# Linear attention and two feed-forward layers on one core: the stores of y1 move from SP's queue to ScalarE's, and the stores of converted weights are written one tile later

## The chip, the cores and the metric

The kernel runs on one core of one Trainium2 chip. The metric is device time of one execution in microseconds, the median of several runs. A core has a matrix engine (TensorE, PE in the rows), a vector engine (VectorE, DVE), a scalar engine (ScalarE, ACT), GpSimd (POOL) and SyncE (SP), which here only issues DMAs. Each engine works through its own queue in order; an instruction that waits holds up all that is queued behind it on the same engine.

## What is computed

The reference, cut to its core:

```python
for t in range(S):                                   # B, H, S, D = 4, 8, 768, 64
    state = gamma[None, :, None, None] * state + np.einsum('bhd,bhe->bhde', k[:, :, t], v[:, :, t])
    y[:, :, t] = scale * np.einsum('bhd,bhde->bhe', q[:, :, t], state)
x = y.transpose(0, 2, 1, 3).reshape(B * S, H * D)    # 3072 tokens of 512
h = x @ w_in                                         # 512 -> 1024
e = np.exp(h - h.max(-1, keepdims=True))
solu = h * e / (e.sum(-1, keepdims=True) + 1e-09)
ln = (solu - mean(solu)) / sqrt(var(solu) + 1e-06) * g_ln
x = ln @ w_out                                       # 1024 -> 512, this is y1
h = x @ w2_in                                        # 512 -> 2048
out = (h * np.cos(h)) @ w2_out                       # 2048 -> 512
```

The weights of the four matrices arrive as 64-bit floats, as pairs of 32-bit words, and are turned into 32-bit floats on the chip.

## The kernel before

Attention is done in 24 steps (two pairs of batches, 12 chunks of 64 positions each). `load_step` issues six loads a step on SP (`kt`, two of `X`, two of `W`, `kn`); `att_prep` scales `kn` on ScalarE in four operations (L223); the rest of a step is short matmuls on TensorE.

The first layer works on tiles of 128 tokens. `mm1` makes `h` in PSUM in two halves of 12 matmuls (L315); there is one buffer for `h`, so the next tile's matmuls wait until the norm has read it. `norm` is a chain over three engines: row maximum on VectorE (L323), exp on ScalarE (L324, tile `u`), `u*h` on VectorE (L325), sum of squares on ScalarE (L328, tile `junk`), small arithmetic on VectorE and GpSimd (L327 to L335, tiles `sm`), and a scaling on ScalarE (L336, tile `u` again). `transp` turns the normed tile by eight transposes on TensorE (L351, tile `tr`, two buffers), and each `tr` is split on ScalarE (`lth`, L354) and VectorE (`ltl`, L355). `mm2` multiplies with the second matrix (48 matmuls, L368) for 256 tokens and half of the 512 outputs; behind every second call a copy on ScalarE (`ys`, L372, one buffer) empties PSUM and a DMA on SP (L373) stores it to `y1d` in DRAM. There are 24 such stores. The second layer reads `y1d` back with `load_y`.

While the first layer runs, the weights of both layers are converted: `load_w` loads a tile of word pairs on SP (`raw`, L155), takes an absolute value on ScalarE (`wt`, L158) and does four operations on VectorE (L161, L162, L164, L167). Tiles of the second layer have no room yet, so `keep` stores them to DRAM on SP (L191, 28 stores, tensors `kept_in` and `kept_out`), and `load_kept` reads them back later. There are two `wt` buffers.

One round of the main loop (`for s in range(EARLY, NG)`) does two tiles of `mm1`, one group of `transp` and `mm2`, one or two attention steps and four calls of `weights`. TensorE's order is the order of the program text. The order on the other engines is set by a scheduler when the program is built, from modelled times; the text gives it only what depends on what.

Of the kernel before, what the change touches and what calls it, by code (L numbers as in the profile page):

```python
# [50 lines left out]
def body(ctx: ExitStack, tc: tile.TileContext, qx, kt, kn, vn, c_sc, c_mg,  # L51
         w_in1, w_out1, gln, w_in2, w_out2, out):
    nc = tc.nc
# [10 lines left out]
    y1d = [dram.tile([128, KD, 512], F32, name=f"y1d{n}") for n in range(NBLK)]  # L64
# [59 lines left out]
    def split(hi, lo, src, pin=False, head=None):  # L124
        op = nc.scalar.activation(out=hi, in_=src if head is None else head, func=AF.Copy)  # L125
        if pin:
            tc.keep_in_program_order(op)
        nc.vector.tensor_tensor(out=lo, in0=src, in1=hi.bitcast(F32), op=ALU.subtract)  # L128
# [13 lines left out]
    def load_w(src, apart=False):  # L142
        seq[0] += 1
        if early:
            raw = early.pop(0)
            src = None
            t = p_boot.tile([128, 512], I32, tag="wt", name="wt", bufs=4)
        elif "lt" not in p2 and seq[0] % 2:
            raw = p2["boot"].tile([128, 512, 2], I32, tag="raw", name="raw", bufs=3)
            t = p2["boot"].tile([128, 512], I32, tag="wt", name="wt", bufs=2)  # L150
        else:
            raw = stg.tile([128, 512, 2], I32, tag="raw", name="raw", bufs=3)
            t = stg.tile([128, 512], I32, tag="wt", name="wt")
        if src is not None:
            nc.sync.dma_start(out=raw, in_=src.rearrange("p (f two) -> p f two", two=2))  # L155
        f = t.bitcast(F32)
        top, low = raw[:, :, 1], raw[:, :, 0]
        first_op = nc.scalar.activation(out=f, in_=top.bitcast(F32), func=AF.Abs)  # L158
        if seq[0] > 2 * KD:
            tc.keep_in_program_order(first_op)  # L160
        nc.vector.tensor_scalar(out=f, in0=f, scalar1=TINY, scalar2=HUGE, op0=ALU.max, op1=ALU.min)  # L161
        nc.vector.tensor_scalar(out=t, in0=t, scalar1=3, scalar2=0x3FFFFFFF,  # L162
                                op0=ALU.logical_shift_left, op1=ALU.bitwise_and)
        nc.vector.scalar_tensor_tensor(out=t, in0=top, scalar=-0x40000000, in1=t,  # L164
                                       op0=ALU.bitwise_and, op1=ALU.bitwise_or)
        full = low if apart else t
        nc.vector.scalar_tensor_tensor(out=full, in0=low, scalar=29, in1=t,  # L167
                                       op0=ALU.logical_shift_right, op1=ALU.bitwise_or)
        return (f, full.bitcast(F32)) if apart else f
# [15 lines left out]
    w2h, w2l = {}, {}  # L185
    kept = {}

    def keep(kind, c, e, k, src):
        if k == 0:
            kept[kind, c, e] = dram.tile([128, 2, 512], F32, name=f"kept_{kind}_{c}_{e}")  # L190
        nc.sync.dma_start(out=kept[kind, c, e][:, k], in_=load_w(src))  # L191

    def load_kept(what, hi, lo):
        t = stg.tile([128, 2, 512], F32, tag="raw", name="raw", bufs=3)
# [164 lines left out]
    def mm2(g, p, e):  # L359
        if e == 0:  # L360
            y1s[g] = p2["pst"].tile([128, 2, 256], F32, tag="y1", name="y1")
        y1 = y1s[g]
        ds = slice((2 * p + e) * 128, (2 * p + e + 1) * 128)
        m = 0
        for j in range(K1):
            lh, ll = lt[g][j // 2]
            for w, a in ((o1[0], lh), (o1[1], lh), (o1[0], ll)):
                nc.tensor.matmul(out=y1[:, e], lhsT=w[:, j, ds], rhs=a[:, j % 2], start=(m == 0), stop=(m == 3 * K1 - 1))  # L368
                m += 1
        if e == 1:  # L370
            ys = moe.tile([128, 2, 256], F32, tag="ys", name="ys", bufs=1)
            nc.scalar.activation(out=ys, in_=y1, func=AF.Copy)  # L372
            nc.sync.dma_start(out=y1d[g // 2][:, 2 * p:2 * p + 2, (g % 2) * 256:(g % 2) * 256 + 256], in_=ys)  # L373


    def load_y(n):
        yh = p2["sb"].tile([128, KD, 512], F32R, tag="yh", name="yh")
        yl = p2["sb"].tile([128, KD, 512], F32R, tag="yl", name="yl")
        for k in range(KD):
            t = p2["sb"].tile([128, 512], F32, tag="yt", name="yt", bufs=2)  # L380
            nc.sync.dma_start(out=t, in_=y1d[n][:, k])
            split(yh[:, k], yl[:, k], t)
        p2["y", n] = (yh, yl)
# [45 lines left out]
    def load_o2(g):  # L429
# [7 lines left out]
        for e in range(2):  # L437
# [4 lines left out]
    wq = [(load_w1, (k, c)) for c in range(2) for k in range(KD)] + [(load_o1, (j,)) for j in range(K1)]  # L442
    wq += [(load_w2, (p_w2a, 0, k)) for k in range(KD)]
    wq += [(keep, ("in", 1, k // 2, k % 2, w_in2[k * 128:(k + 1) * 128, 1024:2048])) for k in range(KD)]
    wq += [(keep, ("out", 0, j // 2, j % 2, w_out2[j * 128:(j + 1) * 128, :])) for j in range(K2)]
    wq += [(keep, ("in", c, k // 2, k % 2, w_in2[k * 128:(k + 1) * 128, c * 1024:(c + 1) * 1024]))
           for c in (2, 3) for k in range(KD)]

    def weights(n):
        for _ in range(n):  # L450
            if wq:
                f, args = wq.pop(0)
                f(*args)
# [83 lines left out]
    for s in range(EARLY, NG):  # L537
        g = s - EARLY
        first(2 * s, 0)
        transp(g, 0)  # L540
        transp(g, 1)
        first(2 * s, 1)
        transp(g, 2)
        transp(g, 3)
        if s < NG - 1:
            attend()
        weights(1)
        for e in range(2):
            mm2(g, 0, e)
        weights(1)  # L550
        first(2 * s + 1, 0)
        first(2 * s + 1, 1)
        weights(1)
        if s % 2 == 0:
            attend()
        for e in range(2):
            mm2(g, 1, e)
        weights(1)
    weights(len(wq))
    load_y(0)  # L560
    nup = 0
    for g in range(NG - EARLY, NG):
        transp(g, 0)
        transp(g, 1)
        up(0, nup)
        transp(g, 2)
        transp(g, 3)
        for e in range(2):
            mm2(g, 0, e)
        load_w2(None, 1 + g - (NG - EARLY), 0)  # L570
        load_o2(g - (NG - EARLY))
        up(0, nup + 1)
        nup += 2
        load_w2(None, 1 + g - (NG - EARLY), 1)
        for e in range(2):
            mm2(g, 1, e)
# [90 lines left out]
```

## Time and profile before

| | us |
|---|---|
| median of 3 runs | 931.36 |
| the runs | 929.67 to 933.35 |
| span of the profiled execution (no other time of it is given) | 932.8 |
| TensorE busy (matmuls) | 893.4 |
| VectorE busy | 622.7 |
| ScalarE busy | 455.5 |
| GpSimd busy | 48.0 |
| chain that ended last, share of TensorE | 84% |

Times within the profile are microseconds from the first instruction. The first layer's main loop runs from about 93 us to 378 us; the y1 stores are issued between 113.8 and 417.5 us. "Idle before" in a row is the time for which the engine had nothing to do ahead of that instruction, with what ended it. A wait is put down to what came last. The y1 stores carry 256 KB each, a weight load 512 KB, a kept store 256 KB.

### The profile page before, as it was taken

To read this page: it belongs to the slowest core of one execution; us is meant where nothing else is said; L and a number is where in the kernel's file an instruction comes from. 1 tells how busy PE (TensorE), PEld (TensorE's weight loads), DVE (VectorE), ACT (ScalarE), POOL (GpSimd) and SP (SyncE) were. 2 spreads that over 40 slices of the span, in tenths; PEclk is the share of its full clock that TensorE was granted. 3 is DMA by queue.
4 is the path that set the end of the run, shared out by engine and by line. 5 is a ranking of instruction groups with operands and counts; after the bars stand their busy time and mean duration, and the time that the engine had idled before them with its cause. 6 is when DMAs were issued, how large, how long until landed. Compare 5 with 4: busy or idle time off the path is not lost.

```text
span 932.8 us, 16044 instructions
## 1 busy us (share of the span) xinstructions
PE 893.4 (96%) x6464; PEld 765.1 (82%) x6464; DVE 622.7 (67%) x1090; ACT 455.5 (49%) x768; POOL 48.0 (5%) x60
## 2 busy tenths in 40 slices
PE   4787999989899999999999999999999999999997
PEld 4676889879799989998888888888888888888886
DVE  6899887587667754566766655756575665656654
ACT  4677666556656555554534333433443343344332
POOL 2112100101011000000000000000000000000000
PEclk7999899989999999999999999999999999999999
DMA  9986354565547422133012002000300030001001
GB/s 260 313 252 194 106 158 146 184 204 161 188 131 226 157 93 90 64 108 111 24 35 56 1 1 73 19 0 1 91 1 1 7 84 1 1 24 45 1 1 46
DMA packets 41884, 85.28 MB, mean 91 GB/s; under 512 B 5457, under 2 KB 11729, under 8 KB 41809
## 3 DMA queue, kind: packets, MB, share of 16 engines
q1 hardware_dynamic: 41376, 83.91, 30.0%
q8 instruction: 51, 0.84, 0.4%
q10 hardware_dynamic: 432, 0.34, 0.1%
q14 instruction: 25, 0.20, 0.1%
HBM read 64.30 MB, written 19.92 MB: 90 GB/s over the span
## 4 chain that ended last, share of the span: by engine, by line
PE 84%; DVE 6%; DMA 5%; ACT 2%; issue 2%; SPq 1%; POOL 0%; DVEq 0%; ACTq 0%
PE h L393 28%; PE acc L418 28%; PE y L368 13%; PE h L315 10%; DMA kn<-kn_dram 3%; PE tr L351 2%; PE y L287 2%; DMA W<-vn_dram 1%; PE sc L230 1%; DVE X L248 1%; DVE wt L164 1%; DVE wt L161 1%; ACT kn L223 1%; ACT junk L328 1%; DVE wt L162 0%
## 5 line engine op out<-in xcount | busy, mean ns | idle before, releaser
L393 PE MATMUL h<-yh,w2h 128*128 128x512 f32 x384 | 149.6, 390 | 0.0
L393 PE MATMUL h<-yl,w2h 128*128 128x512 f32 x384 | 149.4, 389 | 0.0
L393 PE MATMUL h<-yh,w2l 128*128 128x512 f32 x384 | 149.4, 389 | 0.0
L418 PE MATMUL acc<-o2h,gh 128*128 128x512 f32 x384 | 149.4, 389 | 0.0
L418 PE MATMUL acc<-o2h,gl 128*128 128x512 f32 x384 | 149.4, 389 | 0.0
L418 PE MATMUL acc<-o2l,gh 128*128 128x512 f32 x384 | 149.4, 389 | 0.0
L404 ACT ACTIVATE r<-r,hp 128x512 f32<-128x512 f32 x96 | 69.5, 724 | 144.5 <-DVE r L403 144.5
L368 PE MATMUL y<-lth,o1h 128*128 128x256 f32 x384 | 110.2, 287 | 0.0
L368 PE MATMUL y<-ltl,o1h 128*128 128x256 f32 x384 | 108.8, 283 | 0.0
L368 PE MATMUL y<-lth,o1l 128*128 128x256 f32 x384 | 108.6, 283 | 0.0
L401 DVE SCALAR_TENSOR_TENSOR r<-ki,h 128x512 f32<-128x512 int32 x96 | 66.0, 687 | 62.9 <-ACT ki L400 61.9
L405 DVE TENSOR_TENSOR r<-r,h 128x512 f32<-128x512 f32 x96 | 66.0, 687 | 61.6 <-ACT r L404 61.6
L128 DVE TENSOR_TENSOR gl<-r,gh 128x512 fp32r<-128x512 f32 x96 | 66.3, 691 | 45.9 <-ACT gh L125 45.4
L400 ACT ACTIVATE ki<-h 128x512 int32<-128x512 f32 x96 | 57.3, 597 | 74.7 <-PE h L393 74.1
L125 ACT ACTIVATE gh<-r 128x512 fp32r<-128x512 f32 x96 | 60.7, 632 | 65.4 <-DVE r L405 65.4
L393 PEld LDWEIGHTS h<-yh,w2h 128*128 128x128 f32 x384 | 72.1, 188 | 14.9
L418 PEld LDWEIGHTS acc<-o2h,gl 128*128 128x128 f32 x384 | 72.1, 188 | 15.0
L393 PEld LDWEIGHTS h<-yl,w2h 128*128 128x128 f32 x384 | 72.1, 188 | 15.0
L418 PEld LDWEIGHTS acc<-o2l,gh 128*128 128x128 f32 x384 | 72.1, 188 | 14.9
L418 PEld LDWEIGHTS acc<-o2h,gh 128*128 128x128 f32 x384 | 72.0, 188 | 14.9
L393 PEld LDWEIGHTS h<-yh,w2l 128*128 128x128 f32 x384 | 72.1, 188 | 14.8
L315 PE MATMUL h<-w1h,xh 128*128 128x512 f32 x192 | 77.9, 406 | 0.0
(77 smaller groups left out, 1554.3 us busy)
## 6 DMA issues: line engine op xcount, KB each, us to landing
raw<-w_in_dram SPq DMA_DIRECT2D x24, 512.0 KB, 4.4
raw<-w_out_dram SPq DMA_DIRECT2D x24, 512.0 KB, 4.8
kt<-kt_dram SPq DMA_DIRECT2D x24, 256.0 KB, 4.9
X<-qx_dram SPq DMA_DIRECT2D x48, 128.0 KB, 5.0
W<-vn_dram SPq DMA_DIRECT2D x48, 128.0 KB, 4.6
kn<-kn_dram SPq DMA_DIRECT2D x24, 256.0 KB, 5.1
y1d<-ys SPq DMA_DIRECT2D x24, 256.0 KB, 2.1
yt<-y1d SPq DMA_DIRECT2D x24, 256.0 KB, 2.9
```

What stands on the lines that cost most here:

```text
L125: op = nc.scalar.activation(out=hi, in_=src if head is None else head, func=AF.Copy)
L128: nc.vector.tensor_tensor(out=lo, in0=src, in1=hi.bitcast(F32), op=ALU.subtract)
L287: nc.tensor.matmul(out=y[64 * par:64 * par + 64, j], lhsT=d["W"][:, par, j], rhs=d["X"][:, par, j], start=True, stop=True)
L315: nc.tensor.matmul(out=h[:, c], lhsT=a[:, k], rhs=w[:, k, cs], start=(k + m == 0), stop=(k == KD - 1 and m == 2))
L351: nc.tensor.transpose(out=tr[:, e, t * 128:(t + 1) * 128], in_=lns[2 * g + t].rearrange("p c f -> p (c f)")[:, j * 128:(j + 1) * 128], ide ...
L368: nc.tensor.matmul(out=y1[:, e], lhsT=w[:, j, ds], rhs=a[:, j % 2], start=(m == 0), stop=(m == 3 * K1 - 1))
L393: nc.tensor.matmul(out=h, lhsT=w[:, k, cs], rhs=a[:, k], start=(m == 0), stop=(m == 3 * KD - 1))
L400: nc.scalar.activation(out=ki, in_=h, func=AF.Identity, scale=INV2PI, bias=0.25)
L401: nc.vector.scalar_tensor_tensor(out=r, in0=ki, scalar=-C1, in1=h, op0=ALU.mult, op1=ALU.add)
L404: nc.scalar.activation(out=r, in_=r, func=AF.Sin, bias=hp[:, 0:1])
L405: nc.vector.tensor_tensor(out=r, in0=r, in1=h, op=ALU.mult)
L418: nc.tensor.matmul(out=acc, lhsT=a[:, ts_], rhs=w, start=(j == 0 and m == 0), stop=(j == K2 - 1 and m == 2))
```

## The change

The store of y1 is issued by ScalarE, behind the copy `ys` that fills the tile, where SP issued it. And `keep` no longer stores a tile as soon as it is converted: it puts the store on a list, which is emptied at the start of the next call of `keep` and once at the end of the loop.

```diff
+    held = []
+
+    def flush_kept():
+        while held:
+            dst, t = held.pop(0)
+            nc.sync.dma_start(out=dst, in_=t)
+
     def keep(kind, c, e, k, src):
         if k == 0:
             kept[kind, c, e] = dram.tile([128, 2, 512], F32, name=f"kept_{kind}_{c}_{e}")
-        nc.sync.dma_start(out=kept[kind, c, e][:, k], in_=load_w(src))
+        flush_kept()
+        held.append((kept[kind, c, e][:, k], load_w(src)))
...
             nc.scalar.activation(out=ys, in_=y1, func=AF.Copy)
-            nc.sync.dma_start(out=y1d[g // 2][:, 2 * p:2 * p + 2, (g % 2) * 256:(g % 2) * 256 + 256], in_=ys)
+            nc.scalar.dma_start(out=y1d[g // 2][:, 2 * p:2 * p + 2, (g % 2) * 256:(g % 2) * 256 + 256], in_=ys)
...
     weights(len(wq))
+    flush_kept()
     load_y(0)
```

The lines behind the new function stand 8 lower in the changed kernel (L336 is L344, L372 is L380), and a kept store is L193 where it was L191. TensorE's order and GpSimd's are the same in both.

ScalarE at store 5, in the round that runs from 158 us to 192 us, before (the number behind a name tells one buffer or tile from another):

```order
L255 ACTIVATE W<-S 64x512
L256 ACTIVATE W<-S 64x512
L158 ACTIVATE wt<-raw 128x512
L223 ACTIVATE kn<-kn,cs 128x128 x4
L328 ACTIVATE junk,sm_123<-u,sm_123 128x1024
L372 ACTIVATE ys<-y_2125 128x512
L158 ACTIVATE wt<-raw 128x512
L336 ACTIVATE u<-u,sm_123 128x1024
L125 ACTIVATE xh<-x_1566 128x512
```

and now:

```order
L263 ACTIVATE W<-S 64x512
L264 ACTIVATE W<-S 64x512
L158 ACTIVATE wt<-raw 128x512
L231 ACTIVATE kn<-kn,cs 128x128 x4
L336 ACTIVATE junk,sm_123<-u,sm_123 128x1024
L380 ACTIVATE ys<-y_2124 128x512
L344 ACTIVATE u<-u,sm_123 128x1024
L381 DMA y1d_73<-ys 128x2x256
L158 ACTIVATE wt<-raw 128x512
L125 ACTIVATE xh<-x_1566 128x512
```

The second weight conversion (`wt`) stood right behind `ys` and stands now behind `u` and the store. The same move is made at stores 3, 9 and 13 (at 3 the store stands ahead of `u`). At stores 7 and 11 the first of the four `kn` scalings goes ahead of `junk`. On VectorE the split of a `w2` tile changes places with its neighbour three times, and one `ltl` near the end of the loop; all else there stays.

SP in the same round, before:

```order
L191 DMA kept_out_0_2115<-wt 128x512
L373 DMA y1d_73<-ys 128x2x256
L155 DMA raw<-w_out_dram 128x1024
L191 DMA kept_out_0_2115<-wt 128x512
L155 DMA raw<-w_out_dram 128x1024
L91 DMA kt<-kt_dram 128x512
L98 DMA kn<-kn_dram 128x512
```

and now:

```order
L193 DMA kept_out_0_2114<-wt 128x512
L155 DMA raw<-w_out_dram 128x1024
L193 DMA kept_out_0_2114<-wt 128x512
L155 DMA raw<-w_out_dram 128x1024
L91 DMA kt<-kt_dram 128x512
L98 DMA kn<-kn_dram 128x512
```

The y1 store has gone; the kept stores stand where they stood, ahead of the next weight load. With the y1 stores left out, SP's whole queue is the same in both kernels.

## Rows read from the trace of the kernel before

**Rows 1.** The page: the span.

```profile
span 932.8 us, 16044 instructions
```

**Rows 2.** TensorE's waits, 100 to 420 us: total us, times, longest us.

```profile
PE tr L351 <- DVE ltl L355: 7.6, 5, 4.1
```

**Rows 3.** Busy time by stretch: stretch, length, TensorE busy, granted clock, DMA share, GB/s.

```profile
190.00:193.00 3.00, 2.81 (x32) 0.50 0.92 281
250.00:253.00 3.00, 2.46 (x78) 1.00 0.95 287
260.00:420.00 160.00, 160.00 (x1416) 1.00 0.39 123
```

**Rows 4.** SP's waits over the span: total us, times, longest us.

```profile
SPq L373 <- ACT ys L372: 110.4, 20, 10.9
SPq L191 <- DVE wt L167: 74.9, 24, 9.0
```

**Rows 5.** Timeline of SP: start us, us, engine, line, operation, out<-in.

```profile
126.99 0.38 SPq L373 DMA_DIRECT2D y1d<-ys  x1
129.09 0.33 SPq L155 DMA_DIRECT2D raw<-w_in_dram  x1
...
171.96 0.32 SPq L191 DMA_DIRECT2D kept_out<-wt  x1
...
173.33 0.42 SPq L98 DMA_DIRECT2D kn<-kn_dram  x1
...
219.21 0.32 SPq L191 DMA_DIRECT2D kept_out<-wt  x1
...
232.64 0.32 SPq L191 DMA_DIRECT2D kept_out<-wt  x1
```

**Rows 6.** Timeline of ScalarE, its queue included; idle time before in brackets.

```profile
1.17 0.45 ACTq L109 DMA_DIRECT2D cs<-c_sc_dram  x1
...
142.21 0.65 ACT L158 ACTIVATE wt<-raw 128x512 f32<-128x512 f32 x1
143.18 1.25 ACT L336 ACTIVATE u<-u,sm 128x1024 f32<-128x1024 f32 x1 [0.32 <-DVE sm L335]
...
168.30 0.60 ACT L372 ACTIVATE ys<-y 128x512 f32<-128x512 f32 x1
168.79 0.65 ACT L158 ACTIVATE wt<-raw 128x512 f32<-128x512 f32 x1
169.76 1.25 ACT L336 ACTIVATE u<-u,sm 128x1024 f32<-128x1024 f32 x1 [0.32 <-DVE sm L335]
...
181.22 1.28 ACT L223 ACTIVATE kn<-kn,cs 128x128 f32<-128x128 f32 x4 [5.68 <-DMA kn<-kn_dram]
...
226.53 1.29 ACT L223 ACTIVATE kn<-kn,cs 128x128 f32<-128x128 f32 x4 [2.58 <-DMA kn<-kn_dram]
...
241.03 1.28 ACT L223 ACTIVATE kn<-kn,cs 128x128 f32<-128x128 f32 x4 [3.67 <-DMA kn<-kn_dram]
...
257.32 1.15 ACT L328 ACTIVATE junk<-u,sm 128x1024 bf16<-128x1024 f32 x1 [1.49 <-DVE sm L327]
...
259.62 1.29 ACT L223 ACTIVATE kn<-kn,cs 128x128 f32<-128x128 f32 x4 [1.06 <-DMA kn<-kn_dram]
```

**Rows 7.** Timeline of VectorE.

```profile
145.26 1.22 DVE L323 TENSOR_REDUCE sm<-h 128x1 f32<-128x1024 f32 x1
...
156.06 0.69 DVE L355 TENSOR_TENSOR ltl<-tr,lth 128x512 fp32r<-128x512 f32 x1
```

**Rows 8.** Timeline of TensorE: the two gaps.

```profile
190.10 1.11 PE L351 MATMUL tr<-ident,u 128*128 128x128 f32 x4 [4.15 <-DVE ltl L355]
...
249.92 0.66 PE L351 MATMUL tr<-ident,u 128*128 128x128 f32 x4 [1.82 <-DVE ltl L355]
```

**Rows 9.** Chain of waits, 153 to 158 us: start us, us, what.

```profile
153.40 0.87 PE tr L351 x8
154.28 2.74 PE h L315 x12
```

## What the change should do to the time

> **What bounds the kernel now.** The page comes first, for the span of 932.8 us [rows 1]. Then the view of TensorE's waits, which says where a gain or a loss can lie: in all of the stretch in which y1 is stored and weights are kept (113 us to 418 us) TensorE waits only for the second half of a transpose pair, `tr` for `ltl`, 7.6 us in five waits, the longest 4.1 us [rows 2]. The busy times by stretch show the rest: from 260 us on TensorE is busy without a break, so nothing the change does there can gain; it could only open new gaps [rows 3]. Behind the 4.15 us wait that ends at 190.10 TensorE ran at the lower of its two levels (granted 0.50, that is 1.2 GHz, in 190 to 193 us), behind the 1.82 us wait at 249.92 it did not (1.00 in 250 to 253 us) [rows 3, 8]. The whole stake on the gain side is thus 7.6 us of waits and some 1.5 us of slow work (3 us at half speed; an estimate from those rows).
>
> **SP, where the stores leave.** SP's own waits look like a large prize: 110.4 us in 20 waits for `ys` at the y1 store [rows 4]. The timeline of SP takes it back. The store at 126.99 had waited for `ys`, but the next in the queue, the weight load at 129.09, waits for a conversion on VectorE and would have stood there in any case [rows 5]. It is so at each of these stores: behind it stands either a load that needs a buffer or a kept store that needs the end of a conversion (74.9 us in 24 waits [rows 4]). What SP really gets back is 24 issues, 0.38 us each [rows 5]. The Trainium skill, "DMA: Bandwidth & Descriptors", section "Issuing engines are not separate DMA queues", says that starting DMAs from several engines saves only the sequencer's time to start them. By that rule SP's relief is 24 x 0.38 = 9 us of SP's own time and none on the path; by the 110.4 us row alone one would have credited the whole 7.6 us of TensorE's waits, and the queue's order here sides with the rule. I credit nothing.
>
> **The kept stores.** The order of SP shows them where they were, each right ahead of the next weight load; this half moves nothing and costs nothing. The scheduler, not the text, sets that order.
>
> **ScalarE, where the stores go.** Two things happen there. First, each y1 store is an instruction in ScalarE's queue: the issue takes 0.45 us (the three DMAs that ScalarE issues at the start [rows 6]), and it must wait until `ys` is finished, which costs another 0.1 us, since ScalarE otherwise starts the next operation 0.49 us into the 0.60 us copy (168.30 and 168.79). So some 0.6 us for what follows, if it was back to back. Second, the order around it changes, as the two fences on the change show: at four places (stores 3, 5, 9 and 13 of 24) the weight conversion `wt`, which stood right behind `ys`, now stands behind `u` (L336 before), and `u` must wait for a small chain on VectorE and GpSimd. At 142.21 the conversion ran while `u` waited until 143.18; now it starts at 143.18 + 1.15 = 144.33, 2.1 us later. At 168.79 and 169.76 the store is behind `u` as well: 169.76 + 1.25 + 0.45 = 171.45, 2.65 us later [rows 6]. At two more places (stores 7 and 11) one of four `kn` scalings goes ahead of `junk`.
>
> **Who waits for it.** On VectorE the four conversion operations keep their place ahead of the row maximum (L323), which opens the norm chain. At 145.26 L323 began straight behind them, so it begins at 147.3 [rows 7]. The whole chain behind it (exp, `u`, `junk`, then on ScalarE `ys`, `u`, two `wt`, two `lth`) is back to back and shifts by 2.0 us, and with it the two `ltl`, the second of which began at 156.06. TensorE wants the first at 157.02, where its 12 matmuls end, and the second 0.43 us later (half of eight transposes) [rows 7, 9]. The second now ends at 156.06 + 0.69 + 2.0 = 158.75, against 157.45: a new wait of **1.3 us**.
>
> At store 5 there is a second victim. SP's kept store at 171.96 waits for the end of the late conversion, and behind it stand a load, `kt` and `kn`, issued at 173.33; the conversion ends 2.5 us later, so the kept store goes to 174.46 [rows 5]. `kn` is what ScalarE stands for until 181.22 with 5.68 us of idle time [rows 6], and that is the wait behind the 4.15 us gap of TensorE. In other rounds `kn` was used 7.3 us (219.21 to 226.53) to 8.4 us (232.64 to 241.03) after the kept store ahead of it [rows 5, 6]; so here at 181.8 to 182.9, later by 0.6 to 1.7 us. I take 1.1, and 0.2 for the store that stands between `ys` and the second `wt` in the chain behind: **1.3 us**. At store 9 the same: kept store 232.64 to 235.1, `kn` at 242.4 to 243.5 instead of 241.03, middle 1.9, with 0.2: **2.1 us**. That makes a wait of 1.8 into one of 3.9, close to the one after which the clock fell; I count the fall, **1.5 us** as above.
>
> Store 13 repeats store 3 without `kn` (**1.3 us**). Store 11 gets there another way: `junk`, which ran at 257.32, stands behind a `kn` that lands at 259.62 [rows 6]; less what `u` used to wait anyhow and plus the issue, the conversion is 1.8 us late, and the result is that of store 3 (**1.2 us**). At store 7 it is 0.6 us, which the slack there covers. Where only the store comes in between, ScalarE's idle time hides it, save at the first two stores, whose 0.6 us goes straight into the wait that TensorE already has before 130 us (**0.7 us**), and at stores 15 and 16, which leave **0.5 us**. The last eight stores fall where TensorE waits for nothing and ScalarE waits for TensorE; nothing.
>
> **Sum.** 0.7 + 1.3 + 1.3 + 2.1 + 1.5 + 1.2 + 1.3 + 0.5 = 9.9 us, or 8.4 without the clock. The profiled span, 932.8 us, is 1.4 us above the median of the runs, 931.36, and inside their spread of 929.67 to 933.35; the page gives no time of that execution beside its span. I add the difference to the median: **941.3 us**.
>
> **Bounds.** Of the eight terms four are differences of a shift and a slack; with a microsecond more slack in each and no fall of the clock some 4.5 us are left (936). With `kn` at its late ends (1.2 us more), a slow stretch twice as long and a second one, 14.1 us are reached (945.5). The price of an issue on ScalarE in mid-program isn't in the trace; between nothing and twice 0.45 us it moves the sum by about 2 us either way, since the order is what costs.
>
> **Rivals.**
> (a) Hidden: the late conversions are made up before TensorE asks. For it: TensorE waits for nothing after 260 us today [rows 3], so there is slack in many rounds. Against: the `ltl` slack at 157.45 is 0.7 us, less than the 2.0 us that come. Price 0 to 4 us: 931 to 935.5.
> (b) Faster: with the outputs on ScalarE's queue SP runs ahead, `kn` lands before ScalarE wants it, and the waits and the slow clock go: 931.36 - 7.6 - 1.5 = 922. The point that decides is whether `kn` is issued earlier in its round than at 173.33 [rows 5]; against it, the kept store ahead of it in SP's order waits for a conversion that is now later. The Trainium skill, "Perfetto Trace Analysis", section "DMA Optimizations", suggests one DMA-capable engine for inputs and another for outputs, which would be this gain. No row here shows it: after each y1 store the queue waits for VectorE.
> (c) Worse: more of the gaps grow past the length at which the clock falls, each 1.5 us and up, over 946.
> (d) The change does nothing to the order of loads and stores of kept weights. That is half of my reading already and is priced at nothing.
>
> **Chances.** Forecast 0.62, (a) 0.20, (b) 0.08, (c) 0.10. The range 931 to 946 holds the forecast and nearly all of (a), and leaves out (b) and (c). A measurement of this kernel can tell about 0.5% from no change, 4.7 us here: slower by more than that (over 936) 0.70, within it 0.23, faster 0.07.
>
> **What would show it.** Right: in the profile of the changed kernel `tr` waits for `ltl` in eight or more places, some 15 us in all instead of 7.6; ScalarE's conversion at store 5 begins behind `u` and the store; `kn` in that round is issued 2 us or more later after the attention block than before; a stretch at 1.2 GHz near 250 us. The y1 stores show as issues on ScalarE of 0.4 us. Wrong: SP's waits for `ys` gone and `kn` issued earlier, or L323 beginning no later behind the block of matmuls it reads; or the new waits there, but each eaten by a shorter one behind it.

## The result and the profile after

The changed kernel takes 941.84 us (median of 4 runs, 940.99 to 946.14), the kernel before 931.48 us beside it (4 runs, 929.67 to 933.35): a ratio of 1.0125, 95% interval 1.0096 to 1.0154, or 10.4 us more. The forecast was 941.3. One of the ten runs of `e1_hold_only` further down took 2271.66 us and is no part of that kernel's ratio.

The page of the changed kernel, its span and the engines' busy times:

```profile
span 939.6 us, 16035 instructions
...
PE 898.0 (96%) x6464; PEld 767.4 (82%) x6464; DVE 622.7 (66%) x1090; ACT 455.9 (49%) x768; POOL 48.3 (5%) x60
```

No engine got more work; TensorE's 4.6 us more of busy time are the same matmuls at a lower clock (below). TensorE's waits, 100 to 420 us (total us, times, longest us), against 7.6 us in five waits in [rows 2]:

```profile
PE tr L359 <- DVE ltl L363: 11.1, 9, 4.4
PE h L323 <- DVE sm L337: 0.3, 1, 0.3
```

The gaps on TensorE's timeline (start us, us, ..., idle before in brackets), as in [rows 8], and the busy times by stretch (stretch, length, busy, granted clock, DMA share, GB/s), as in [rows 3]:

```profile
130.01 0.66 PE L359 MATMUL tr<-ident,u 128*128 128x128 f32 x4 [1.49 <-DVE ltl L363]
...
192.40 0.91 PE L359 MATMUL tr<-ident,u 128*128 128x128 f32 x4 [4.42 <-DVE ltl L363]
...
253.29 0.66 PE L359 MATMUL tr<-ident,u 128*128 128x128 f32 x4 [2.42 <-DVE ltl L363]
...
312.14 1.25 PE L359 MATMUL tr<-ident,u 128*128 128x128 f32 x8 [0.99 <-DVE ltl L363]
...
407.90 1.25 PE L359 MATMUL tr<-ident,u 128*128 128x128 f32 x8 [0.40 <-DVE ltl L363]
```

```profile
130.00:140.00 10.00, 9.71 (x144) 0.83 0.69 204
...
253.00:256.00 3.00, 2.16 (x24) 0.68 0.77 270
260.00:420.00 160.00, 158.61 (x1412) 1.00 0.38 120
```

Two gaps are new (312 and 408 us, in a stretch that had none), two have grown (130 and 253 us), and behind both of those TensorE now works for a while at the lower of its two levels (1.2 GHz: granted 0.50 from 132 to 134 us and from 255 to 257 us; the means of 0.83 and 0.68 mix it with 2.4 GHz). The 192 us gap is hardly longer than in [rows 8].

On SP the waits for `ys` of [rows 4] are gone. In their place SP stands before the kept stores (over the span; 74.9 us in 24 waits and 5.5 us in 3 before):

```profile
SPq L193 <- DVE wt L167: 116.0, 25, 11.1
...
SPq L193 <- DVE wt L162: 29.0, 3, 12.1
```

ScalarE's timeline at stores 2 and 5, its queue included; the row to compare for store 5 is 168.30 to 169.76 in [rows 6]:

```profile
126.57 0.59 ACT L380 ACTIVATE ys<-y 128x512 f32<-128x512 f32 x1
127.19 0.38 ACTq L381 DMA_DIRECT2D y1d<-ys  x1
127.62 0.68 ACT L158 ACTIVATE wt<-raw 128x512 f32<-128x512 f32 x1 [0.46 <-ACT ys L380]
...
169.14 0.60 ACT L380 ACTIVATE ys<-y 128x512 f32<-128x512 f32 x1
170.90 1.24 ACT L344 ACTIVATE u<-u,sm 128x1024 f32<-128x1024 f32 x1 [1.16 <-DVE sm L343]
170.92 0.39 ACTq L381 DMA_DIRECT2D y1d<-ys  x1
172.05 0.65 ACT L158 ACTIVATE wt<-raw 128x512 f32<-128x512 f32 x1
...
183.26 1.28 ACT L231 ACTIVATE kn<-kn,cs 128x128 f32<-128x128 f32 x4 [4.60 <-DMA kn<-kn_dram]
```

Two different costs stand here. At store 2 the conversion begins 1.05 us after the copy began, where 0.49 us was usual [rows 6], since the issue waits for the copy's end. At store 5 the issue runs during `u` and delays nothing by itself: the conversion follows 1.15 us behind the start of `u`, as an operation behind `u` does without a store. But it comes 2.9 us after the copy's start, where it came 0.49 us after.

**Where the time went.** TensorE's order is the same in all kernels of this case, and its transposes make 24 blocks, so the interval from the start of one block to the next can be compared across kernels. In the best kernel below (`e7_kn_late`), whose `tr` waits are 0.7 us in 100 to 420 us, nearly every interval has its least value; the table gives what each profiled execution took beyond that one, in us, summed over the intervals that each pair of y1 stores bears on. One entry as an example: from the block at 130.01 us to the next, at 155.01, after took 25.00 us, `e7_kn_late` 23.52 (130.49 to 154.01), so 1.48 of the 3.0 in the first column. Some labels are shortened.

```
                            stores  1-2  3-4  5-6  7-8  9-10 11-12 13-14 15-16 17-24   sum
order of before:  before            0.4  0.0  6.6  0.0  2.8  0.0   0.0   0.0   0.0    9.8
                  e1_hold_only     -0.2  0.0  4.4  0.0  2.1  0.0   0.0   0.0   0.0    6.3
                  e5_no_store      -0.5  0.0  1.2  0.0  2.5  0.0   0.0   0.0   0.0    3.1
                  e6_pin_copy       0.1  0.0  1.2  0.0  5.5  0.0   0.0   0.0   0.6    7.4
order of change:  after             3.0  0.2  6.6  0.8  4.7  0.1   1.3   0.1   0.6   17.4
                  e2_y1_only        2.5  0.7  6.4  0.5  6.8  0.0   1.1   0.1   0.6   18.6
mean of two less mean of four       2.8  0.5  3.1  0.6  2.5  0.0   1.2   0.1   0.4   11.4
parts:            e3_order_back     2.8  0.2  5.2  0.0  2.4  0.1   0.0   0.3   0.6   11.5
                  e4_order_only     1.2  0.8  7.0  0.0  3.9  0.8   1.2   0.0   0.0   14.9
                  e10_conv_5_9     -0.5  0.0  5.8  0.0  2.9  0.0   0.0   0.0   0.0    8.2
                  e11_conv_3_13     0.9  0.8  2.6  0.0  4.4  0.0   0.4   0.0   0.0    9.1
                  e12_kn_square     0.1  0.0  2.7  0.8  4.9  0.0   0.0   0.0   0.0    8.6
kn late:          e8 (and pin)      0.4  0.0  0.0  0.0  0.0  0.0   0.0   0.0   0.6    0.9
                  e9 (and change)   2.8  0.0  2.3  0.8  3.1  0.8   1.4   0.1   0.6   11.7
```

The count begins at the second block. Ahead of it the executions differ by up to 4.6 us (first block at 92.41 to 96.99 us) without a pattern, and behind the last block all are alike (531.7 us in before, after and `e7_kn_late`). Columns 5-6 and 9-10 scatter by 5 and 3 us between executions of one and the same order; the others repeat within 1 us.

The pairs are not quite clean. Where a conversion is late, TensorE can also wait with its next `h`, and that wait falls in the interval that is counted to the pair before. So most of the 1.2 and 0.9 us of `e4_order_only` and `e11_conv_late_3_13` in column 1-2 belongs to store 3 (waits of 0.60 us at 150.68 and 0.47 us at 153.32), and some 1.0 of the 2.7 us of `e12_kn_before_square` in column 5-6 to store 7 (0.65 us at 207.79).

### The profile page after: what moved, and what is told of

It reads as the page before. It is cut to its first block, busy times and chain, and to the rows that moved or that the text cites. A ratio compares the mean times of both kernels' runs of the same rounds, so it can differ in the third digit from the quotient of the medians.

```text
span 939.6 us, 16035 instructions
## 1 busy us (share of the span) xinstructions
PE 898.0 (96%) x6464; PEld 767.4 (82%) x6464; DVE 622.7 (66%) x1090; ACT 455.9 (49%) x768; POOL 48.3 (5%) x60
## 4 chain that ended last, share of the span: by engine, by line
PE 69%; DVE 13%; DMA 6%; ACT 5%; issue 4%; SPq 1%; POOL 1%; ACTq 0%; DVEq 0%
PE acc L426 28%; PE h L401 28%; PE y L376 6%; DMA kn<-kn_dram 4%; PE h L323 4%; DVE wt L164 2%; PE tr L359 1%; DVE wt L161 1%; DVE X L256 1%; DVE sm L331 1%; ACT wt L158 1%; DVE u L333 1%; DMA W<-vn_dram 1%; PE sc L238 1%; DVE ltl L363 1%
```

## The experiments

Ties below are ordering edges: they set which of two instructions stands first in ScalarE's queue and make nothing wait. `behind("u", 6, "wt", 21)` puts scaling pass 6 (L336) behind conversion 21 (L158), each counted from 0; `kn` counts single scalings (L223), `junk` the Square passes (L328). Except where said, the order of all other work is that of the kernel named. The kernel before had a median of 931.46, 930.82 and 931.13 us beside the three groups of four. The ratios on record are not quotients of these medians and differ from them by up to 0.2% (`e7_kn_late`: 925.68 / 930.82 is 0.9945), so a cost worked out from a ratio is good to some 2 us.

| run | median us | ratio to before | 95% |
|---|---|---|---|
| `e1_hold_only` | 930.80 | 0.9993 | 0.9976 to 1.0010 |
| `e2_y1_only` | 942.93 | 1.0130 | 1.0098 to 1.0161 |
| `e3_order_back` | 935.68 | 1.0057 | 1.0034 to 1.0079 |
| `e4_order_only` | 940.28 | 1.0099 | 1.0068 to 1.0130 |
| `e5_no_store` | 931.72 | 1.0004 | 0.9979 to 1.0029 |
| `e6_pin_copy` | 929.58 | 0.9992 | 0.9964 to 1.0020 |
| `e7_kn_late` | 925.68 | 0.9926 | 0.9906 to 0.9946 |
| `e8_kn_late_pin_copy` | 925.28 | 0.9928 | 0.9906 to 0.9950 |
| `e9_kn_late_change` | 937.27 | 1.0072 | 1.0047 to 1.0098 |
| `e10_conv_late_5_9` | 934.25 | 1.0036 | 1.0019 to 1.0053 |
| `e11_conv_late_3_13` | 934.56 | 1.0035 | 1.0008 to 1.0062 |
| `e12_kn_before_square` | 933.45 | 1.0025 | 1.0003 to 1.0047 |

### The two halves

```diff
 # e1_hold_only: the change, but
-            nc.scalar.dma_start(out=y1d[g // 2][...], in_=ys)
+            nc.sync.dma_start(out=y1d[g // 2][...], in_=ys)
 # e2_y1_only: the change, but
-        flush_kept()
-        held.append((kept[kind, c, e][:, k], load_w(src)))
+        nc.sync.dma_start(out=kept[kind, c, e][:, k], in_=load_w(src))
```

> Only the half that holds the kept stores back by one tile; the y1 stores stay on SyncE. The instruction order of every engine is then that of before. Theory ORDER (the change costs because the y1 issue on ScalarE let other work slip ahead of weight conversions and ahead of the Square pass): 931.5, ratio 1.000 within 0.003. Theory ISSUE (the change costs the time that ScalarE spends on issuing): 931.5 too. Theory HOLD (the held store itself delays kn's scalings): 933 to 935.

> Only the half that moves the y1 stores to ScalarE; kept stores are not held by name, but their order on SyncE is that of after. Theories ORDER and ISSUE: all of the loss, 941 to 942, ratio 1.010 to 1.013. Theory HOLD: 937 to 939.

0.9993 and 1.0130: the held stores do nothing, and the whole loss comes with the y1 store's move. HOLD is out.

### Order or issue

```diff
 # e3_order_back: the change, and
+    behind("u", 6, "wt", 21); behind("u", 8, "wt", 25); behind("u", 12, "wt", 33); behind("u", 16, "wt", 41)
+    for j, b in ((10, 68), (14, 80)):
+        for a in range(4):
+            behind("kn", b + a, "junk", j)
+    behind("xh", 7, "w2h", 1); behind("W", 23, "w2h", 3)
 # e4_order_only: the kernel before, and
+    behind("wt", 21, "u", 6); behind("wt", 25, "u", 8); behind("wt", 33, "u", 12); behind("wt", 41, "u", 16)
+    behind("junk", 10, "kn", 68); behind("junk", 14, "kn", 80)
+    behind("w2h", 1, "xh", 7); behind("w2h", 3, "W", 23)
```

> The whole change, y1 issued by ScalarE directly behind its copy, but ScalarE's other work tied back into the order that it had before: at stores 3, 5, 9 and 13 (counted from 1) the weight conversion stands ahead of the last normalising pass again, at two attention steps the Square pass ahead of the kn scalings, and the two early swaps are undone. Theory ORDER: 932 to 935, nearly all of the loss gone. Theory ISSUE (0.37 us of issue and some 0.1 us of waiting for the own copy at each of 16 stores): 940 to 942, as the whole change.

> The kernel before, all stores on SyncE, nothing issued by ScalarE, but ScalarE's work tied into the order that the change gave it. Theory ORDER: 938 to 942. Theory ISSUE: 931.5, ratio 1.000 within 0.003.

The order alone, with every store still on SP, costs 9.2 us of the 10.4 (931.46 x 0.0099). ORDER holds for the larger part. But putting it back leaves 5.3 us, more than ORDER allowed and less than ISSUE asked for: with the issue directly behind the copy at all 16 stores of the loop there is a cost of its own. The two don't add up to the whole, since in the changed order some of the issues stand behind `u`, where they cost nothing (store 5 above). The table says where the 5.3 us sit: 2.8 at stores 1 and 2, 0.6 at the end, and the rest cannot be told from the scatter of columns 5-6 and 9-10.

> The whole change, but the weight conversion is tied behind the y1 copy itself and no longer behind the issue that follows it. ScalarE's work then stands in the order of before, and at 11 of the 16 stores in the loop the issue stands behind the conversion or behind the last normalising pass, where the copy has ended and the issue runs beside an activation. Theory ORDER: 931 to 933. Theory ISSUE, with the stall of the copy's own end hidden: 931 to 934; if the issue costs its 0.37 us wherever it stands: 935 to 938, as with the order put back alone (935.7).

```diff
 # e6_pin_copy: the change, and in load_w
         if seq[0] > 2 * KD:
-            tc.keep_in_program_order(first_op)
+            pin_behind_work(first_op)       # the same, but passes over the y1 issues
```

0.9992: the whole loss is gone, with all 24 stores on ScalarE. This also shows why the order had moved. `load_w` pins its first operation behind whatever the text last put on ScalarE. That was the copy `ys`; with the change it is the store's issue, which is ready later, and the scheduler filled the time with `u`. Pinned to the copy, the conversion comes first again and the issue mostly falls behind it. ScalarE's timeline at store 2 in this kernel:

```profile
128.44 0.58 ACT L388 ACTIVATE ys<-y 128x512 f32<-128x512 f32 x1
128.91 0.67 ACT L166 ACTIVATE wt<-raw 128x512 f32<-128x512 f32 x1
129.05 0.38 ACTq L389 DMA_DIRECT2D y1d<-ys  x1
```

The conversion follows 0.47 us behind the copy's start, as before the change, and the issue runs beside it. Against 1.05 us that is the price of an issue straight behind its own copy: 0.58 us. The rival reading, 0.37 us wherever it stands, is out.

### Which of the moves

> The kernel before, all stores on SyncE; only at stores 5 and 9 the weight conversion is tied behind the last normalising pass. These are the two stores behind which kn is waited for with 5.68 and 3.67 us. If the way through kept store and kn carries the loss: 935 to 938, over half of the 9.2 us of the order alone. If not: 931 to 933.

> The kernel before with the same tie at stores 3 and 13 alone, where no long wait for kn follows. Way through kn: 931 to 933. Way through VectorE, the conversion's other steps in front of the next norm: 934 to 936 (the prediction's 1.3 us at each, and clock).

> The kernel before with one kn scaling ahead of the Square pass at two attention steps, as the change has it, and the conversions where they were. The scaling takes 0.39 us and may wait for kn, by 0.67 and 1.06 us where the four stand behind the Square pass now: 931 to 933, at most 1 us a place; over 934 if that place, and not the conversions, carries the loss of the order.

```diff
 # e10_conv_late_5_9: the kernel before, and
+    behind("wt", 25, "u", 8); behind("wt", 33, "u", 12)
 # e11_conv_late_3_13: the kernel before, and
+    behind("wt", 21, "u", 6); behind("wt", 41, "u", 16)
 # e12_kn_before_square: the kernel before, and
+    behind("junk", 10, "kn", 68); behind("junk", 14, "kn", 80)
```

The three cost 3.4, 3.3 and 2.3 us (ratio less one, times 931.13), 9.0 together, against 9.2 for all at once: the loss of the order is spread over the three pairs of places. Stores 5 and 9 do not carry most of it, as the way through `kn` would have it. Two of the three miss what was expected of them: `e10_conv_late_5_9` lies between its two readings, and `e12_kn_before_square` a little above 1 us a place. The three intervals are wide, so the split is known to about 2 us each; for `e12_kn_before_square` the interval all but reaches 1.

What the places have in common is a late conversion ahead of the row maximum. With a scaling ahead of the Square pass it comes about through `kn`: the scaling waits for its DMA, behind it stand the Square pass, `u`, `ys` and the conversion, the maximum begins straight behind the conversion's last step, and TensorE's next `h` waits for the norm (`e12_kn_before_square`, ScalarE, VectorE, TensorE):

```profile
196.19 0.40 ACT L232 ACTIVATE kn<-kn,cs 128x128 f32<-128x128 f32 x1 [4.45 <-DMA kn<-kn_dram]
...
203.32 0.69 DVE L176 SCALAR_TENSOR_TENSOR wt<-raw,wt 128x512 int32<-128x512 int32 x1
203.93 1.22 DVE L332 TENSOR_REDUCE sm<-h 128x1 f32<-128x1024 f32 x1
...
207.79 0.47 PE L324 MATMUL h<-w1h,xh 128*128 128x512 f32 x1 [0.65 <-DVE sm L338]
```

In before this maximum had waited for its matmuls:

```profile
207.08 1.22 DVE L323 TENSOR_REDUCE sm<-h 128x1 f32<-128x1024 f32 x1 [1.10 <-PE h L315]
```

At store 3 of `e11_conv_late_3_13`, which issues nothing on ScalarE and waits for `kn` as long as before does (2.64 and 2.65 us), the same is seen:

```profile
148.85 0.69 DVE L176 SCALAR_TENSOR_TENSOR wt<-raw,wt 128x512 int32<-128x512 int32 x1
149.46 1.22 DVE L332 TENSOR_REDUCE sm<-h 128x1 f32<-128x1024 f32 x1
...
153.32 0.47 PE L324 MATMUL h<-w1h,xh 128*128 128x512 f32 x1 [0.47 <-DVE sm L338]
```

### SP without the stores

```diff
 # e5_no_store: the kernel before, but
-            nc.sync.dma_start(out=y1d[g // 2][...], in_=ys)
...
-            nc.sync.dma_start(out=t, in_=y1d[n][:, k])
+            nc.sync.dma_start(out=t, in_=qx[n % 2, 4 * (n // 2) + k])
```

> The kernel before without any y1 store: the SyncE queue loses all 24 of them and nothing takes their place, ScalarE keeps its order; the up stage reads tiles of the same size from the input qx in place of y1, so the output is of another activation. This is the most that freeing SyncE of the y1 stores can give. Rival (b) of the prediction (weight loads and kn come earlier, TensorE's waits shrink): 922 to 926. The reading that the wait of SyncE only moves to the kept stores, whose tiles come no earlier: 930 to 932.

1.0004. With no y1 store at all on SP, its waits for kept stores grow from 74.9 us [rows 4] to this:

```profile
SPq L191 <- DVE wt L167: 105.1, 25, 11.1
```

and the kept store is at 169.47, 17.35 us behind the round's first transposes at 152.12, where it was 18.72 us behind (171.96 in [rows 5], 153.24 in the trace of before) and 17.45 us in `e1_hold_only`, which has all its stores on SP. `kn` is issued 19.78 us behind them, and just as far behind in `e1_hold_only`. Rival (b) is out: SP's 110.4 us before the stores were worth nothing.

### The wait for kn

```diff
 # e7_kn_late: the kernel before, and   (e8: e6_pin_copy, and)
+    for b, n in ((56, 6), (60, 8), (64, 9), (72, 12), (76, 13), (84, 16)):
+        for a in range(NHP):
+            behind("kn", b + a, "u", n)
```

> The kernel before, all stores on SyncE, but at six attention steps the four kn scalings, for whose DMA ScalarE waited 2.0 to 5.7 us ahead of a norm, are tied behind that norm's last pass. If kn's wait on ScalarE is what makes the norm, the transposes' splits and so TensorE late at the 4.15 us and 1.82 us waits of before: 7.6 us of waits and the slow-clock stretch behind the longer one go, 921 to 926. If the lateness lies in the norm chain itself, or the kn scalings now delay the attention: 930 to 935.

> The whole change with the conversion tied behind the copy and the kn scalings behind the norm's last pass, as in the two runs ahead of it. If both hold: 921 to 926, the same as with the kn scalings alone. If the store's issue on ScalarE costs by itself, 3 to 5 us more than those alone.

0.9926 and 0.9928: both are 0.7% better than the kernel before (0.6% by the medians), and alike. In [rows 6] ScalarE stands 5.68 us before `kn`, with a norm queued behind it whose input was there. In `e7_kn_late` the same scalings stand behind that norm's last pass and wait for nothing:

```profile
179.98 1.24 ACT L345 ACTIVATE u<-u,sm 128x1024 f32<-128x1024 f32 x1 [1.11 <-DVE sm L344]
181.13 0.65 ACT L167 ACTIVATE wt<-raw 128x512 f32<-128x512 f32 x1
181.68 1.27 ACT L232 ACTIVATE kn<-kn,cs 128x128 f32<-128x128 f32 x4
```

TensorE's waits there, 100 to 420 us, and its busy time and granted clock in that stretch:

```profile
PE tr L360 <- DVE ltl L364: 0.7, 2, 0.4
...
100.00:420.00 320.00, 319.28 (x3147) 1.00 0.47 151
```

So the waits and the slow stretches of before come from `kn`'s place in ScalarE's queue, not from the y1 stores. The runs also scatter less: 923.3 to 926.8 us, where before runs from 924.9 to 936.0 in its groups here.

> The whole change, the issue directly behind the copy and the weight conversion behind the last normalising pass as the change has it, and only the kn scalings of six attention steps tied behind that pass (and behind the conversion). If the late conversion hurts because it delays the kept store, with it the load of kn, and with that kn's scalings, which stand ahead of a norm: the loss goes with the wait for kn, 925 to 929. If the conversion behind the norm's pass hurts by itself (VectorE gets its part of the conversion later, in the way of the next norm): 933 to 937, that is, kn late gains its 5 us and the 10 us of loss stay.

```diff
 # e9_kn_late_change: the change, and the ties of e7_kn_late, and to keep the rest as the change has it
+    for b, w in ((56, 21), (60, 25), (72, 33), (84, 41)):
+        for a in range(4):
+            behind("kn", b + a, "wt", w)
+    for j, b in ((10, 68), (14, 80)):
+        for a in (1, 2, 3):
+            behind("kn", b + a, "junk", j)
+    behind("ys", 6, "u", 10); behind("ys", 10, "u", 14)
```

937.3 us, just above the upper end of the second reading. Taking `kn` out of the way gains some 5 us on the changed kernel as well, but 11.6 us separate its median from that of `e7_kn_late`. Not all of this is the late conversion. 3.4 us stand in columns 1-2 and 17-24 and are the issue's, as in `e3_order_back`. At stores 7 and 11 a scaling still stands ahead of the Square pass and waits for `kn` (3.79 us at 200.81, 4.54 us at 260.18). And at store 6 the issue stands straight behind its copy and holds up the splits that follow, ScalarE and TensorE:

```profile
189.45 0.66 ACT L167 ACTIVATE wt<-raw 128x512 f32<-128x512 f32 x1 [0.44 <-ACT ys L389]
...
191.38 0.66 PE L368 MATMUL tr<-ident,u 128*128 128x128 f32 x4 [0.61 <-DVE ltl L372]
```

What is left for the late conversion at stores 5, 9 and 13 is at most 0.8, 0.8 and 1.4 us, in which the issues behind it have a share; this run does not part the two. It does show that there is a loss at these stores without a wait for `kn`, and that its way runs through VectorE. At store 9 of this kernel, ScalarE and VectorE:

```profile
232.27 1.25 ACT L353 ACTIVATE u<-u,sm 128x1024 f32<-128x1024 f32 x1 [1.44 <-DVE sm L352]
...
233.42 0.64 ACT L167 ACTIVATE wt<-raw 128x512 f32<-128x512 f32 x1
```

```profile
235.75 0.69 DVE L176 SCALAR_TENSOR_TENSOR wt<-raw,wt 128x512 int32<-128x512 int32 x1
236.36 1.22 DVE L340 TENSOR_REDUCE sm<-h 128x1 f32<-128x1024 f32 x1
```

The row maximum begins straight behind the conversion's last step, with no idle time. In `e7_kn_late` the conversion was done early and the maximum waited for the matmuls (0.85 us idle before it). The chain behind the maximum passes the delay on, as the prediction had it: at store 5 the maximum begins 16.06 us behind the round's first transposes (14.66 in `e7_kn_late`), and exp, Square pass and `u` are each 1.4 us later too.

## Why the prediction came out right, point by point

**SP gets nothing back: right.** `e5_no_store` is 1.0004, and `e6_pin_copy` 0.9992. The rule of the Trainium skill that the prediction weighed ("DMA: Bandwidth & Descriptors", section "Issuing engines are not separate DMA queues") agrees with both. The suggestion of the Trainium skill, "Perfetto Trace Analysis", section "DMA Optimizations", that an engine of their own for outputs may make sense brought no gain in any run here (0.9992 for `e6_pin_copy`; 925.28 us for `e8_kn_late_pin_copy` against 925.68 for `e7_kn_late`).

**The kept stores cost nothing: right** (`e1_hold_only`).

**An issue takes 0.45 us, and some 0.6 us for what follows: right in sum.** It takes 0.37 to 0.39 us, and straight behind the copy it moves the next operation by 0.58 us. That it also adds its time behind `u` was wrong: at store 5 issue and `u` overlap. The conversion there is nevertheless 2.9 us behind the copy's start (3.15 were forecast), because `u` came later.

**Stores 1 and 2, 0.7 us: too small.** The step that failed is the clock, which the prediction counted at store 9 alone. The wait grew as forecast, from 0.83 us (in the trace of before, at 129.72 us) to 1.49, but TensorE fell to 1.2 GHz behind it, another 1.5 us in the interval after. Here the issue itself does it, not the order: `e3_order_back` has the same 2.8 us, `e6_pin_copy` 0.1.

**Store 3, 1.3 us: mechanism right, but little of it is left in the changed kernel.** The row maximum and the second `ltl` came as late as forecast:

```profile
147.76 1.22 DVE L331 TENSOR_REDUCE sm<-h 128x1 f32<-128x1024 f32 x1
...
158.52 0.68 DVE L363 TENSOR_TENSOR ltl<-tr,lth 128x512 fp32r<-128x512 f32 x1
```

That is 2.5 us behind [rows 7] each. But TensorE had itself become 1.8 us later at store 2, so 0.2 us were left (0.7 in `e2_y1_only`). Where store 2 is not late the whole term shows, 1.7 us in `e4_order_only` and 1.6 in `e11_conv_late_3_13`, in good part as a wait of `h`, which the prediction did not name. The terms were added as if each met the slack of before, while a loss at one store is slack at the next.

**Store 5, 1.3 us: kept store and `kn` late as forecast; what that costs is known only roughly.** The two in the round:

```profile
175.09 0.33 SPq L193 DMA_DIRECT2D kept_out<-wt  x1
...
176.48 0.38 SPq L98 DMA_DIRECT2D kn<-kn_dram  x1
```

`kn` is issued 21.47 us behind the round's first transposes (155.01), against 20.09 in before and 19.78 in `e1_hold_only` and `e6_pin_copy`. What the prediction could not know is that 4.15 us was a long wait for before: its `kn` took 7.9 us from issue to use (173.33 to 181.22 in [rows 5, 6]), in `e5_no_store` 4.2 us:

```profile
171.90 0.38 SPq L98 DMA_DIRECT2D kn<-kn_dram  x1
```

```profile
176.14 1.28 ACT L223 ACTIVATE kn<-kn,cs 128x128 f32<-128x128 f32 x4 [2.05 <-DMA kn<-kn_dram]
```

So the two profiles compared alone show no growth at this store. Between executions there is one: the four with this conversion late have 5.8 to 7.0 us in that column (after, `e2_y1_only`, `e4_order_only`, `e10_conv_late_5_9`), the seven others that wait for `kn` 1.2 to 6.6, some 3 us less on the mean. How much of it comes through `kn` and how much through VectorE stays open; `e9_kn_late_change` keeps 0.8 us in the interval behind store 5 with no wait for `kn` (the rest of its 2.3 belongs to store 7).

**Store 7, nothing: wrong by 0.6 us or more,** the scaling ahead of the Square pass (`e12_kn_before_square`, 0.8, and some 1.0 ahead of it).

**Store 9, 2.1 and 1.5 us of clock: the slow stretch came, the wait hardly grew.** It went from 1.82 to 2.42 us, where 3.9 was forecast. Column 9-10 grows by 1.9 us between the two profiles and 2.5 on the mean, of 3.6 forecast. By itself that is not shown: executions of the order of before scatter by 3 us there, some with a slow stretch of their own, and `e10_conv_late_5_9` has 2.9.

**Store 11, 1.2 us: wrong for the changed kernel,** 0.0 to 0.1 us there and in `e2_y1_only`. `e4_order_only` and `e9_kn_late_change` have 0.8, and a wait of `h` just before (0.54 us at 273.44, 1.26 us at 272.40). In the first two TensorE had come out of a slow stretch shortly before and was late already, so this may again be a loss that serves as slack; no run tests it. **Store 13, 1.3 us: right** (1.3 and 1.1; 0.4 in `e11_conv_late_3_13`). **The last 0.5 us: right in size,** but at the transposes at 408 us, not at stores 15 and 16.

**The base.** The prediction took before's profiled execution to be 1.4 us above the median, by its span. In the runs of the kernel before beside the experiments the time of an execution is 1.7 to 3.4 us above its own span (after: 941.4 and 939.6), so it was rather 3 us or more above. Span against span the change costs 6.8 us, run against run 10.4. That the sum of 9.9 us hit the runs so closely is luck in part: terms too large (stores 3, 9 and 11) and too small (1, 2, 7 and, as far as it is known, 5) made up for each other.

**The signs.** As named, `tr` waits in nine places, the conversion at store 5 begins behind `u`, the issues take 0.4 us and TensorE works at 1.2 GHz near 250 us. Two signs were too strong: the waits add up to 11.1 us, not 15, and `kn` at store 5 is issued 1.4 us later in its round, not 2 or more.

**The rivals.** (a), hidden, falls by `e4_order_only`: the late conversions are not made up. (b) falls by `e5_no_store`. (c) did not come, though one run of four took 946.14 us. (d) was half of the reading and holds.

## What to carry to other kernels

An instruction that only issues a DMA still has a place in a compute engine's queue, and an ordering rule that means "behind the last work" takes it for work: after such a move, compare the engine's order, and tie to the operation that was meant. Put the issue where its producer has ended and something else runs, and no cost was measured (0.9992). A wait on a queue that only issues (110 us here) is worth nothing if the next in the queue would wait anyway; six waits for a DMA on a compute engine, the longest 5.68 us with a norm behind it whose input was there, were worth 0.7% together. And before a term is measured against a wait, see that wait in more than one execution.

## What the hardware showed

**The issue overlaps.** ScalarE issued a DMA while an activation ran (170.92 beside 170.90, 129.05 beside 128.91); it stood still where the DMA had to wait for the operation right ahead (0.46 us at 127.62).

**The clock does not follow the wait's length alone.** It fell behind a 1.49 us wait (130.01 us in after), and behind this one in `e6_pin_copy`, TensorE's timeline and the 3 us after it:

```profile
246.64 0.66 PE L367 MATMUL tr<-ident,u 128*128 128x128 f32 x4 [1.86 <-DVE ltl L371]
```

```profile
247.00:250.00 3.00, 2.46 (x47) 0.54 0.95 292
```

but not behind a longer one in `e4_order_only`:

```profile
251.71 0.66 PE L360 MATMUL tr<-ident,u 128*128 128x128 f32 x4 [2.13 <-DVE ltl L364]
```

```profile
252.00:255.00 3.00, 2.46 (x86) 1.00 0.95 290
```

**The same load lands at very different times:** `kn` of one round (store 5) was used 7.9 us after its issue in before and 6.4 in `e1_hold_only`, 6.8 in after and 4.3 in `e6_pin_copy`, each two with one order on SP. With this wait out of the way the runs scatter by 3.5 us (`e7_kn_late`), those of before in the same group by 8.7.
